# One fused attention and MLP kernel: its opening reordered, its queries computed one unit sooner, its V rows loaded in longer runs

## The chip, the cores and the metric

The kernel runs on one core of one Trainium2 chip. The metric is the device time of one execution in microseconds (us). The kernel before was run three times without the profiler: 1286.58, 1287.96 and 1288.90 us, median 1287.96. One more execution was taken by the hardware profiler; its time was 1287.13 us, and the span from its first to its last instruction 1285.4 us. All rows of the profile are from that execution.

## The reference, cut to what matters

```python
xn = layernorm(x)                                   # x: 2048 tokens x 512
# attention branch: 32 heads of 128, 2048 cached keys
q = (xn @ wq) split into heads
p = softmax((q @ k_cache.T) * 128 ** -0.5)          # per head, 2048 x 2048
s = (p @ v_cache) joined @ wo                       # 2048 x 512
# MLP branch, on the same xn
h  = gelu(layernorm(xn) @ w1); four column groups of h shifted by -1, +1, -2, +2 tokens
x1 = xn + shifted @ w2
g  = silu(x1 + gelu(layernorm(x1) @ w3) @ w4)
out = x + s * g
```

Inputs and output are bf16. Softmax is invariant to the order of the keys, as long as K and V use the same order.

## The kernel before, in words

**Tiling.** Attention is cut into 128 units. A unit is one head and 512 queries; the units run in groups of four heads, and inside a group over the four blocks of 512 queries, with the four heads innermost. So units 0 to 3 use tokens 0 to 511, units 4 to 7 tokens 512 to 1023, units 8 to 11 tokens 1024 to 1535, and units 12 to 15 tokens 1536 to 2047; then the next four heads start. A unit has eight slots. Slot number n counts through all units, so unit u begins with slot 8u. In each slot TensorE multiplies two blocks of 128 keys by the 512 queries (`s_slot`, L181, tile `ps_s`, two buffers), ScalarE takes the exponential of the 1024 results in one instruction (L191, tile `pT`), and TensorE does two matmuls of the exponentials with V for the slot five earlier (`pv_slot`, L210, tile `ps_o`). VectorE adds the eight exponential tiles of a unit (`add_first` L197, `add_next` L202, the folds L207 and L208), and TensorE turns that sum into the softmax denominators in slot 3 of the next unit (`sums`, tile `ps_sum`, four matmuls of one column). The reciprocal goes to DRAM and comes back spread over all partitions (`dr`, `rb`), and `norm` (L258) scales the unit's output.

**Queries.** `q_mm` (L165) makes the 512 queries of one unit: four matmuls from the transposed tokens `xnT` and the head's query weights `wq_h` into the PSUM tile `ps_q`; `q_copy` (L173) brings them to SBUF as `qT`. Units 1 to 3 get theirs during unit 0. From unit 3 on, unit u computes the queries of unit u + 1: two matmuls in its first slot, two in its second, the copy in its third.

**Tokens.** x is loaded in 16 tiles of 128 tokens. `ln1_stats` (L343) and `ln1_apply` (L360) normalise one tile: statistics on VectorE, a reciprocal square root on GpSimd (L117, L118), the scaling on VectorE (L355), then a DMA transpose issued by SyncE that writes the tile's part of `xnT`. The four tiles of the first 512 tokens are transposed on TensorE instead, by matmuls with an identity (`first_tokens`, L365). The other tiles have a fixed slot each for their statistics and their scaling, in two lists at L628 and L629: tiles 8 to 11 are scaled in slots 29, 37, 45 and 47, tiles 12 to 15 in slots 53, 61, 69 and 77.

**Order.** Every engine's instructions keep the order in which the program writes them (`pin`); there is no planner. Work tied to a slot is put into a list (`at`) and is written at the end of that slot. So an instruction that waits holds up all that stands behind it on its engine, and the DMAs issued by SyncE (SP) go out in one queue: K pieces (DMA transposes, four for each head), V halves, `dr`, `rb`, and the token transposes. The MLP branch is cut into 136 chunks that are spread over units 5 to 119. The output projection (`wo_mm`, tile `ps_wo`) takes four matmuls in a unit. In PSUM, `ps_q`, `ps_sum` and `ps_wo` share one buffer, and the MLP's `ps_m` has another.

**The end.** The last four token tiles' output projections go to four halves of two two-bank PSUM tiles, `pa` and `pb` (L738 to L740); each is scaled (L302), added (L307) and stored.

Of the kernel before, what the change touches and what calls it, by code (L numbers as in the profile page):

```python
# [17 lines left out]
def kernel(  # L18
# [15 lines left out]
    nc = tc.nc  # L34
# [77 lines left out]
    def mm(out, lhsT, rhs, start, stop):  # L112
        pin(nc.tensor.matmul(out=out, lhsT=lhsT, rhs=rhs, start=start, stop=stop))  # L113
# [15 lines left out]
    def at(n, fn):  # L129
        todo[n].append(fn)  # L130
# [16 lines left out]
                in_=A_k_cache[0, h, i * w:(i + 1) * w, :], transpose=True))  # L147

    def load_v(h, halves):
        v = A_v_cache[0, h].rearrange("(kc p) d -> p kc d", p=P)  # L150
        for i in halves:
            if i == 0:
                vBs[h] = vp.tile([P, KC, Dh], BF16, name="vb")
            ks = slice(i * KC // 2, (i + 1) * KC // 2)
            pin(nc.sync.dma_start(out=vBs[h][:, ks, :], in_=v[:, ks, :]))
# [9 lines left out]
    def q_mm(u, dcs):  # L165
        g, qt, hh = units[u]
        if dcs[0] == 0:
            st[u] = dict(psq=psX.tile([P, 512], FP32, tag="xa", name="ps_q"))
        for dc in dcs:
            mm(st[u]["psq"][:], wqs[g * HG + hh][:, dc, :],  # L170
               xnT[:, dc, qt * 512:(qt + 1) * 512], dc == 0, dc == DC - 1)

    def q_copy(u):  # L173
        qT = qtp.tile([P, 512], BF16, name="qT")
        if u > QUIET:
            pin(nc.scalar.activation(out=qT[:], in_=st[u].pop("psq")[:], func=ACT.Identity))
        else:
            pin(nc.vector.tensor_copy(out=qT[:], in_=st[u].pop("psq")[:]))  # L178
        st[u]["qT"] = qT

    def s_slot(u, p):  # L181
        g, qt, hh = units[u]
        s = st[u]
        sps = psS.tile([P, 2, 512], FP32, name="ps_s")
        for j in range(2):
            kc = 2 * p + j
            mm(sps[:, j, :], kTs[g * HG + hh][:, kc * P:(kc + 1) * P], s["qT"][:], True, True)
# [3 lines left out]
        pin(nc.scalar.activation(  # L191
            out=s["pT"][-1][:, jj:jj + 2, :], in_=sps[:], func=ACT.Exp, scale=SCALE))
# [167 lines left out]
    def ln1_apply(t):  # L360
        xn = ln1_norm(t)
        pin(nc.sync.dma_start_transpose(out=xnT[:, :, t * P:(t + 1) * P], in_=xn[:]))
        pin(nc.gpsimd.dma_start(out=xn_d[t][:], in_=xn[:]))

    def first_tokens():  # L365
        xns = [ln1_norm(t) for t in range(4)]
        st[0] = dict(psq=psX.tile([P, 512], FP32, tag="xa", name="ps_q"))
        psq = st[0]["psq"]
        for t in range(4):
            tp = psO.tile([P, DC, P], FP32, tag="ps_o", name="ps_o")  # L370
# [3 lines left out]
            pin(nc.scalar.activation(out=xnT[:, :, ts], in_=tp[:], func=ACT.Identity))  # L374
            if t >= 1:
                q_part(t - 1, psq)
        q_part(3, psq)
        qT = qtp.tile([P, 512], BF16, name="qT")
        pin(nc.vector.tensor_copy(out=qT[:, 0:3 * P], in_=psq[:, 0:3 * P]))
        pin(nc.vector.tensor_copy(out=qT[:, 3 * P:], in_=psq[:, 3 * P:]))  # L380
        st[0].pop("psq")
        st[0]["qT"] = qT
        for t in range(4):
            pin(nc.gpsimd.dma_start(out=xn_d[t][:], in_=xns[t][:]))

    def q_part(t, psq):
        ts = slice(t * P, (t + 1) * P)
        for dc in range(DC):
            mm(psq[:, ts], wqs[0][:, dc, :], xnT[:, dc, ts], dc == 0, dc == DC - 1)
# [223 lines left out]

    for t, eng in enumerate([nc.sync, nc.scalar, nc.sync, nc.scalar]):
        ln1_load(t, eng)
    for h in range(HG):
        load_w(h, nc.scalar)
    load_k(0, range(KSPLIT))
    load_v(0, (0, 1))
    load_k(1, range(KSPLIT))  # L620
    for t in range(4):
        ln1_stats(t)
    for t in range(4, 8):
        ln1_load(t, nc.gpsimd)
    first_tokens()
    load_v(1, (0, 1))
    load_k(2, (0, 1))
    for t, stats, apply in zip(range(4, NT), (2, 5, 8, 13, 23, 31, 39, 39, 47, 55, 63, 71),  # L628
                               (4, 7, 12, 15, 29, 37, 45, 47, 53, 61, 69, 77)):  # L629
        if t >= 8:  # L630
            at(stats - 8, lambda t=t: ln1_load(t, nc.gpsimd))
        at(stats, lambda t=t: ln1_stats(t))
        at(apply, lambda t=t: ln1_apply(t))
    for h, slots, halves in ((2, (2, 4), (9, 13)), (3, (5, 7, 14, 16), (21, 22))):
        for i, n in enumerate(slots):
            at(n, lambda h=h, i=i + KSPLIT - len(slots): load_k(h, (i,)))
        for i, n in enumerate(halves):
            at(n, lambda h=h, i=i: load_v(h, (i,)))
    at(28, ph1_load)
    at(64, w2_load)  # L640
    for h in range(HG):
# [146 lines left out]
```

## Time and profile before

| what | value |
|---|---|
| runs without profiler | 1286.58, 1287.96, 1288.90 us |
| profiled execution, its own time | 1287.13 us |
| span of the profiled execution | 1285.4 us |
| VectorE (DVE) busy | 1015.0 us, 79% of the span |
| ScalarE (ACT) busy | 1114.1 us, 87% |
| GpSimd (POOL) busy | 145.0 us, 11% |
| V halves (256 KB), issue to landing | 5.1 us median |
| K pieces, issue to landing | 5.0 us median |
| token transposes, issue to landing | 3.8 us median |

A busy share is a mean over the whole span. Matmul ends are modelled, so in a full stream one matmul of 512 columns shows as 379 ns, while the starts are about 216 ns apart. Where a row of the timeline merges several equal instructions, its first number is the start of the first one. What ended the idle time before an instruction stands in square brackets.

### The profile page before, as it was taken

How to read it: one execution, taken by the hardware profiler on the slowest of the kernel's cores; microseconds unless marked ns; L12 is line 12 of the kernel's file. 1: busy time of each engine (PE TensorE's matmuls, PEld its weight loads, DVE VectorE, ACT ScalarE, POOL GpSimd, SP SyncE). 2: the span in 40 equal slices, each digit the busy share in tenths (PEclk: the TensorE clock that was granted, in tenths of full speed). 3: DMA queues.
4: the chain of work that ended last, by engine and by line, in shares of the span. 5: the costliest groups of instructions: out<-in, count | busy, mean ns of one | idle time of the engine just before them, and what ended most of it. 6: DMA issues, size and time to landing. Idle time of an engine off the chain costs nothing.

```text
span 1285.4 us, 17152 instructions
## 1 busy us (share of the span) xinstructions
PE 1256.3 (98%) x6148; PEld 578.2 (45%) x6272; DVE 1015.0 (79%) x1390; ACT 1114.1 (87%) x1195; POOL 145.0 (11%) x253
## 2 busy tenths in 40 slices
PE   6999999999999999999999999999999999999998
PEld 3444444444444444444444444444444444444443
DVE  5888888888778777788787778887777888777895
ACT  5899998888999988899998889998888999888983
POOL 4432002333111110000001000000000000000110
PEclk9999999999999999999999999999999999999999
DMA  8645454366432554224464246622545224562522
GB/s 180 152 95 111 81 80 79 88 137 133 99 79 77 99 107 88 53 67 83 80 96 80 50 79 95 103 45 62 99 86 86 40 62 76 94 107 54 139 68 54
DMA packets 224791, 113.89 MB, mean 89 GB/s; under 512 B 192641, under 2 KB 201345, under 8 KB 224705
## 3 DMA queue, kind: packets, MB, share of 16 engines
q1 hardware_dynamic: 213056, 85.51, 36.2%
q0 software_dynamic: 9248, 26.49, 8.1%
q8 instruction: 49, 0.80, 0.3%
q10 hardware_dynamic: 2400, 0.79, 0.3%
q14 instruction: 38, 0.30, 0.1%
HBM read 82.58 MB, written 9.70 MB: 72 GB/s over the span
## 4 chain that ended last, share of the span: by engine, by line
PE 82%; ACT 9%; DVE 5%; issue 2%; DMA 1%; POOL 1%; SPq 0%; DVEq 0%; ACTq 0%; POOLq 0%
PE ps_s L113 30%; PE ps_o L113 28%; PE ps_m L113 9%; PE ps_wo L113 7%; PE ps_q L113 7%; ACT pT L191 6%; DVE acc L202 2%; ACT sq L399 1%; PE ps_sum L113 1%; ACT pre L429 1%; DVE acc L207 1%; DMA xin<-in_A_x_dram 0%; DMA kT<-in_A_k_cache_dram 0%; ACT sq L408 0%; DMA rb<-dr 0%
## 5 line engine op out<-in xcount | busy, mean ns | idle before, releaser
L191 ACT ACTIVATE pT<-ps_s 128x1024 bf16<-128x1024 f32 x1024 | 1012.9, 1030 | 145.5 <-PE ps_s L113 139.4
L113 PE MATMUL ps_s<-qT,kT 128*128 128x512 bf16 x2007 | 600.7, 379 | 4.5 <-ACT pT L191 0.9
L113 PE MATMUL ps_o<-pT,vb 128*128 128x512 bf16 x2007 | 599.7, 379 | 4.0 <-DMA vb<-in_A_v_cache_dram 1.6
L202 DVE TENSOR_TENSOR acc<-acc,pT 128x2048 bf16<-128x2048 bf16 x254 | 309.8, 1219 | 60.2 <-ACT pT L191 54.6
L113 PEld LDWEIGHTS <-vb 128*128 128x128 bf16 x2048 | 199.5, 98 | 243.3 <-DMA vb<-in_A_v_cache_dram 2.1
L113 PEld LDWEIGHTS <-kT 128*128 128x128 bf16 x2048 | 196.2, 98 | 239.2 <-issue 21.0
L197 DVE TENSOR_TENSOR acc<-pT 128x2048 bf16<-128x2048 bf16 x128 | 155.8, 1217 | 32.4 <-ACT pT L191 32.1
L113 PE MATMUL ps_q<-xnT,wq_h 128*128 128x512 bf16 (+1 forms) x512 | 151.4, 379 | 1.6 <-ACT xnT L374 0.9
L113 PE MATMUL ps_wo<-wo_h,oT 128*128 128x512 bf16 x450 | 134.8, 379 | 0.9 <-DVE rc L230 0.3
L325 DVE TENSOR_TENSOR s_acc<-ps_wo,s_acc 128x512 f32<-128x512 f32 x100 | 68.9, 689 | 80.3 <-PE ps_wo L113 74.8
L258 DVE TENSOR_TENSOR oT<-ps_o,rb 128x512 bf16<-128x512 f32 x129 | 87.2, 677 | 5.9 <-DMA rb<-dr 5.9
L207 DVE TENSOR_TENSOR acc<-acc 128x1024 bf16<-128x1024 bf16 x127 | 87.9, 692 | 4.3
L178 DVE CAST qT<-ps_q 128x512 bf16<-128x512 f32 x121 | 82.9, 685 | 3.9 <-PE ps_q L113 3.9
L113 PEld LDWEIGHTS <-wq_h 128*128 128x128 bf16 x524 | 51.8, 100 | 62.2 <-issue 3.1
L113 PEld LDWEIGHTS <-oT 128*128 128x128 bf16 x480 | 46.9, 98 | 58.2 <-issue 3.2
L113 PE MATMUL ps_m<-xn2T,w_sb 128*128 128x512 bf16 x217 | 65.0, 378 | 0.3
L113 PE MATMUL ps_m<-w_sb,h2T 128*128 128x512 bf16 x219 | 62.9, 379 | 0.3
L548 POOL DMA_DIRECT2D w_sb<-in_B_w_dram x28 | 21.1, 755 | 353.1 <-PE ps_m L113 313.2
L208 DVE TENSOR_TENSOR acc<-acc 128x512 bf16<-128x512 bf16 x127 | 54.0, 425 | 4.3
L230 DVE RECIPROCAL rc<-ps_sum 128x4 f32<-128x4 f32 x128 | 22.9, 179 | 37.7 <-PE ps_sum L113 36.9
L113 PEld LDWEIGHTS <-acc 128*128 128x128 bf16 x516 | 37.1, 116 | 34.7 <-DVE acc L208 6.6
L580 POOL DMA_DIRECT2D g_d<-xr x16 | 8.7, 546 | 343.0 <-DVE xr L578 343.0
(67 smaller groups left out, 595.0 us busy)
## 6 DMA issues: line engine op xcount, KB each, us to landing
rb<-dr SPq DMA_DIRECT2D x128, 256.0 KB, 4.4
vb<-in_A_v_cache_dram SPq DMA_DIRECT2D x64, 256.0 KB, 5.1
w_sb<-in_B_w_dram POOLq DMA_DIRECT2D x28, 256.0 KB, 4.2
wo_h<-in_A_wo_dram SPq DMA_DIRECT2D x32, 128.0 KB, 4.2
wq_h<-in_A_wq_dram SPq DMA_DIRECT2D x28, 128.0 KB, 4.5
kT<-in_A_k_cache_dram SPq DMA_TRANSPOSE x128, 5.0
xn_d<-xn POOLq DMA_DIRECT2D x16, 128.0 KB, 3.6
dr<-rc SPq DMA_DIRECT2D x128, 2.0 KB, 1.5
```

Source lines behind the costliest of these rows:

```text
L113: pin(nc.tensor.matmul(out=out, lhsT=lhsT, rhs=rhs, start=start, stop=stop))
L178: pin(nc.vector.tensor_copy(out=qT[:], in_=st[u].pop("psq")[:]))
L191: pin(nc.scalar.activation(out=s["pT"][-1][:, jj:jj + 2, :], in_=sps[:], func=ACT.Exp, scale=SCALE))
L197: pin(nc.vector.tensor_tensor(out=s["acc"][:], in0=s["pT"][0][:], in1=s["pT"][1][:], op=ALU.add))
L202: pin(nc.vector.tensor_tensor(out=a[:], in0=a[:], in1=st[u]["pT"][i][:], op=ALU.add))
L207: pin(nc.vector.tensor_tensor(out=a[:, 0:2, :], in0=a[:, 0:2, :], in1=a[:, 2:4, :], op=ALU.add))
L208: pin(nc.vector.tensor_tensor(out=a[:, 0, :], in0=a[:, 0, :], in1=a[:, 1, :], op=ALU.add))
L230: pin(nc.vector.reciprocal(out=rc[:], in_=ps[:]))
L258: pin(nc.vector.tensor_tensor(out=oTs[(g, qt)][:, hh, c], in0=s["o"][:, c], in1=s["rb"][:, c], op=ALU.mult))
L325: pin(nc.vector.tensor_tensor(out=sa, in0=ps[:], in1=sa, op=ALU.add))
L399: pin(nc.scalar.activation(out=sq[:], in_=pre[:], func=ACT.Square, scale=GELU_A ** 0.5))
L548: pin(nc.gpsimd.dma_start(out=w[:], in_=w3_v[:, :, fc * P:(fc + 2) * P]))
```

## The change

- ScalarE gets a first activation on one column right after its two loads of x.
- The query weights of heads 0 to 3 are loaded by GpSimd's queue, three of them before the statistics and one after, instead of by ScalarE's queue.
- TensorE starts with 48 matmuls of 128 columns of the identity with itself, into a score buffer.
- The four first token tiles are all transposed before any query matmul. Their copies out of PSUM are shared between ScalarE and VectorE, the last two tiles use score buffers, the first unit's queries lie in two PSUM tiles, and their copy is split between ScalarE and VectorE. The four stores of the normalised tiles go to slots 9 to 12.
- Statistics and scaling of token tiles 5 to 7 move to slots 5, 8, 11 and 9, 12, 14. The slots of tiles 8 to 15 stay.
- The K pieces of head 3 go to slots 11, 15, 17 and 19, the V halves of heads 2 and 3 to slots 11, 13 and 19, 20.
- From unit 3 on, unit u computes the queries of unit u + 2. Unit 4's queries are made in the last two slots of unit 2. The query weights of the next heads are loaded one unit sooner.
- V is read so that one partition holds four keys that follow each other in memory (1024 bytes instead of 256), and the score matmuls take every fourth column of K as their weights, so that both have the same key order.
- At the end the fourth projection goes to a PSUM tile of its own.

```diff
     def load_v(h, halves):
-        v = A_v_cache[0, h].rearrange("(kc p) d -> p kc d", p=P)
+        v = A_v_cache[0, h].rearrange("(i p j) d -> p i j d", p=P, j=KJ)
...
-            mm(sps[:, j, :], kTs[g * HG + hh][:, kc * P:(kc + 1) * P], s["qT"][:], True, True)
+            kv = kTs[g * HG + hh].rearrange("d (i p j) -> d i j p", p=P, j=KJ)
+            mm(sps[:, j, :], kv[:, kc // KJ, kc % KJ, :], s["qT"][:], True, True)
...
+    def warm_up(n):
+        wt = psS.tile([P, 2, 512], FP32, name="ps_s")
+        for _ in range(n):
+            mm(wt[:, 0, 0:P], ident[:], ident[:], True, True)
+
     def first_tokens():
         xns = [ln1_norm(t) for t in range(4)]
...
+        for t in range(3):
+            turn(t)
+            if t < 2:
+                back(t, (0, DC), True)
+            else:
+                back(t, (0, DC), False)
+        turn(3)
+        back(3, (0, 2), False)
+        back(3, (2, DC), True)
+        for t in range(3):
+            q_part(t)
+        pin(nc.scalar.activation(out=qT[:, 0:3 * P], in_=qA[:, 0:3 * P], func=ACT.Identity))
+        q_part(3)
+        pin(nc.vector.tensor_copy(out=qT[:, 3 * P:], in_=qB[:, 3 * P:]))
...
-    for h in range(HG):
-        load_w(h, nc.scalar)
+    act1 = const.tile([P, 1], FP32, name="act1")
+    pin(nc.scalar.activation(out=act1[:], in_=nhalf[:], func=ACT.Identity))
+    for h in range(HG - 1):
+        load_w(h, nc.gpsimd)
     load_k(0, range(KSPLIT))
     load_v(0, (0, 1))
     load_k(1, range(KSPLIT))
+    warm_up(WARM)
...
-    for t, stats, apply in zip(range(4, NT), (2, 5, 8, 13, 23, 31, 39, 39, 47, 55, 63, 71),
-                               (4, 7, 12, 15, 29, 37, 45, 47, 53, 61, 69, 77)):
+    for t, stats, apply in zip(range(4, NT), (2, 5, 8, 11, 23, 31, 39, 39, 47, 55, 63, 71),
+                               (4, 9, 12, 14, 29, 37, 45, 47, 53, 61, 69, 77)):
...
-            at((b + (-3, -3, 0, 0)[hh]) * SPU + (5, 7)[hh % 2], lambda h=h: load_w(h))
+            at((b + (-4, -4, -1, -1)[hh]) * SPU + (5, 7)[hh % 2], lambda h=h: load_w(h))
...
-        if p in (0, 1) and HG - 1 <= u < NU - 1:
-            q_mm(u + 1, (2 * p, 2 * p + 1))
+        if u == HG - 2 and p in (6, 7):
+            q_mm(HG, (2 * p - 12, 2 * p - 11))
+        if u == HG - 2 and p == 7:
+            q_copy(HG)
+        if p in (0, 1) and HG - 1 <= u < NU - 2:
+            q_mm(u + 2, (2 * p, 2 * p + 1))
...
-        if p == 2 and HG - 1 <= u < NU - 1:
-            q_copy(u + 1)
+        if p == 2 and HG - 1 <= u < NU - 2:
+            q_copy(u + 2)
...
-    dst = [(pa, pa, pb, pb)[j][:, j % 2, :] for j in range(4)]
+    pc = psX.tile([P, D], FP32, tag="xa", name="ps_wo")
+    dst = [pa[:, 0, :], pa[:, 1, :], pb[:, 0, :], pc[:]]
```

More of the change, by code (lines that the diff above doesn't have):

```diff
@@ L56 @@
     KSPLIT = 4
+    KJ = KC // KSPLIT
     BASE_J = [3, 3, 2, 2]
@@ L59 @@
     PADW = 8
+    WARM = 48
     PSUM = bass.MemoryType.PSUM
@@ L153, in load_v @@
                 vBs[h] = vp.tile([P, KC, Dh], BF16, name="vb")
-            ks = slice(i * KC // 2, (i + 1) * KC // 2)
-            pin(nc.sync.dma_start(out=vBs[h][:, ks, :], in_=v[:, ks, :]))
+            ks = slice(i * KSPLIT // 2, (i + 1) * KSPLIT // 2)
+            pin(nc.sync.dma_start(
+                out=vBs[h].rearrange("p (i j) d -> p i j d", j=KJ)[:, ks], in_=v[:, ks]))
     def load_w(h, eng=nc.sync):
@@ L167, in q_mm @@
         if dcs[0] == 0:
-            st[u] = dict(psq=psX.tile([P, 512], FP32, tag="xa", name="ps_q"))
+            st[u] = dict(psq=psX.tile([P, 512], FP32, tag="xm" if u == HG else "xa", name="ps_q"))
         for dc in dcs:
@@ L174, in q_copy @@
         qT = qtp.tile([P, 512], BF16, name="qT")
-        if u > QUIET:
+        if u > QUIET + 1:
             pin(nc.scalar.activation(out=qT[:], in_=st[u].pop("psq")[:], func=ACT.Identity))
@@ L363, in ln1_apply, with turn @@
         pin(nc.gpsimd.dma_start(out=xn_d[t][:], in_=xn[:]))
+    def warm_up(n):
+        wt = psS.tile([P, 2, 512], FP32, name="ps_s")
+        for _ in range(n):
+            mm(wt[:, 0, 0:P], ident[:], ident[:], True, True)
     def first_tokens():
         xns = [ln1_norm(t) for t in range(4)]
[L367 to L370, printed above, removed]
+        st[0] = {}
+        qA = psX.tile([P, 512], FP32, tag="xa", name="ps_q")
+        qB = psX.tile([P, 512], FP32, tag="xm", name="ps_q")
+        qT = qtp.tile([P, 512], BF16, name="qT")
+        st[0]["qT"] = qT
+        tps = []
+        def turn(t):
+            if t < 2:
+                tp = psO.tile([P, DC, P], FP32, tag="ps_o", name="ps_o")[:]
+            else:
+                tp = psS.tile([P, 2, 512], FP32, name="ps_s")[:, 0, :].rearrange("p (c q) -> p c q", c=DC)
@@ L371, in first_tokens @@
             for dc in range(DC):
                 mm(tp[:, dc, :], xns[t][:, dc * P:(dc + 1) * P], ident[:], True, True)
-            ts = slice(t * P, (t + 1) * P)
[L374 to L380, printed above, removed]
@@ L381, in first_tokens, with back @@
-        st[0].pop("psq")
-        st[0]["qT"] = qT
-        for t in range(4):
[L384 to L389, printed above, removed]
+            tps.append(tp)
+        def back(t, dcs, on_act):
+            dst = xnT[:, dcs[0]:dcs[1], t * P:(t + 1) * P]
+            src = tps[t][:, dcs[0]:dcs[1], :]
+            if on_act:
+                pin(nc.scalar.activation(out=dst, in_=src, func=ACT.Identity))
+            else:
+                pin(nc.vector.tensor_copy(out=dst, in_=src))
@@ new lines, in q_part @@
+        def q_part(t):
+            ts = slice(t * P, (t + 1) * P)
+            psq = qB if t == 3 else qA
+            for dc in range(DC):
+                mm(psq[:, ts], wqs[0][:, dc, :], xnT[:, dc, ts], dc == 0, dc == DC - 1)
+        for t in range(3):
+            turn(t)
+            if t < 2:
+                back(t, (0, DC), True)
+            else:
+                back(t, (0, DC), False)
[4 more added lines that the diff above has]
+            q_part(t)
@@ L392 @@
+        pin(nc.scalar.activation(out=qT[:, 0:3 * P], in_=qA[:, 0:3 * P], func=ACT.Identity))
+        q_part(3)
+        pin(nc.vector.tensor_copy(out=qT[:, 3 * P:], in_=qB[:, 3 * P:]))
+        for t in range(4):
+            at(9 + t, lambda t=t: pin(nc.gpsimd.dma_start(out=xn_d[t][:], in_=xns[t][:])))
     mlp = {}
@@ L620 @@
     load_k(1, range(KSPLIT))
+    warm_up(WARM)
     for t in range(4):
         ln1_stats(t)
+    load_w(HG - 1, nc.gpsimd)
     for t in range(4, 8):
@@ L633 @@
         at(apply, lambda t=t: ln1_apply(t))
[L634 to L638, printed above, removed]
+    for n, h, piece in ((2, 2, 2), (4, 2, 3), (11, 3, 0), (15, 3, 1), (17, 3, 2), (19, 3, 3)):
+        at(n, lambda h=h, piece=piece: load_k(h, (piece,)))
+    for n, h, half in ((11, 2, 0), (13, 2, 1), (19, 3, 0), (20, 3, 1)):
+        at(n, lambda h=h, half=half: load_v(h, (half,)))
     at(28, ph1_load)
@@ L664 @@
             pv_slot(*divmod(m, SPU))
-        if u == 0 and p in (0, 2, 4):
+        if u == 0 and p in (1, 3, 5):
             q_mm(1 + p // 2, range(DC))
-        if u == 0 and p in (1, 3, 5):
-            q_copy(1 + p // 2)
-        if p in (0, 1) and HG - 1 <= u < NU - 1:
-            q_mm(u + 1, (2 * p, 2 * p + 1))
+        if u == 0 and p in (2, 4, 6):
+            q_copy(p // 2)
+        if u == HG - 2 and p in (6, 7):
[4 more added lines that the diff above has]
+            q_mm(u + 2, (2 * p, 2 * p + 1))
         if p == 0 and u >= 1:
             add_last(u - 1)
-        if p == 2 and HG - 1 <= u < NU - 1:
-            q_copy(u + 1)
+        if p == 2 and HG - 1 <= u < NU - 2:
+            q_copy(u + 2)
         if p == 2 and u >= 2:
```

## The prediction

> **What bounds the kernel now.** I read the page's busy shares first, then a table of windows, then the timeline where the windows lose time.
>
> ```profile
> PE 1256.3 (98%) x6148; PEld 578.2 (45%) x6272; DVE 1015.0 (79%) x1390; ACT 1114.1 (87%) x1195; POOL 145.0 (11%) x253
> ```
>
> ```profile
> 0.00:10.00 10.00, 1.69 (x15) 1.53 (x16) 4.83 (x15) 2.37 (x3) 5.11 (x16) 1.00 0.87 178
> 10.00:20.00 10.00, 8.78 (x40) 4.49 (x39) 2.92 (x6) 5.05 (x6) 3.66 (x8) 1.00 1.19 244
> 20.00:30.00 10.00, 8.91 (x45) 3.83 (x43) 8.67 (x14) 8.89 (x11) 4.19 (x6) 1.00 0.63 138
> 40.00:60.00 20.00, 18.33 (x90) 8.29 (x91) 16.39 (x28) 17.40 (x20) 7.72 (x20) 1.00 0.60 146
> 60.00:80.00 20.00, 19.66 (x97) 8.97 (x97) 17.90 (x28) 18.34 (x21) 6.97 (x9) 1.00 0.46 98
> 320.00:640.00 320.00, 317.95 (x1553) 146.24 (x1582) 251.56 (x330) 287.70 (x312) 25.64 (x43) 1.00 0.41 83
> ```
>
> The columns after the window are the busy us of PE, weight loads, DVE, ACT and POOL, the granted clock, the DMA share and GB/s. From 60 us on PE is short of nothing (317.95 of 320). So the time is PE's work plus what PE loses before 60 us and at the end: whatever PE waits less in the opening is gained in full, and a wait put in later is lost in full.
>
> ```profile
> 7.40 1.28 ACT L374 ACT_TABLE_LOAD   x1 [7.40 <-DMA kT<-in_A_k_cache_dram]
> 13.33 1.01 PE L113 MATMUL ps_s<-qT,kT 128*128 128x512 bf16 x2 [0.85 <-DVE qT L380]
> 14.13 1.91 PE L113 MATMUL ps_q<-xnT,wq_h 128*128 128x512 bf16 x4
> 15.84 1.91 PE L113 MATMUL ps_s<-qT,kT 128*128 128x512 bf16 x4
> 17.55 1.09 PE L113 MATMUL ps_q<-xnT,wq_h 128*128 128x512 bf16 x4
> 19.10 8.36 ACT L191 ACTIVATE pT<-ps_s 128x1024 bf16<-128x1024 f32 x9 [0.23 <-PE ps_s L113]
> 27.79 0.29 PE L113 MATMUL ps_sum<-ones_t,acc 128*128 128x1 bf16 x4 [1.09 <-DVE acc L208]
> 36.40 0.29 PE L113 MATMUL ps_sum<-ones_t,acc 128*128 128x1 bf16 x4 [1.15 <-DVE acc L208]
> 47.55 0.60 PE L113 MATMUL ps_o<-pT,vb 128*128 128x512 bf16 x2 [1.57 <-DMA vb<-in_A_v_cache_dram]
> ```
>
> The first score matmul stands at 13.33. From there to 17.55 a matmul takes (15.84 - 14.13) / 4 = 0.427 us, later 0.216, though the clock column says 1.00: PE starts at half rate. The Trainium skill ("TensorE: Matmul & The Clock Gate", Part 1) has the clock at half until about 3.4 us of sustained work; the full-rate row at 17.55 agrees, 4.2 us after 13.33. Then come three waits, two for a unit's sum and one for V of head 3.
>
> The price of the query change is read further on. Slots 44 to 47 carry, behind scores and PV, two projection and two MLP pairs; the next query pair is the first of slot 48.
>
> ```profile
> 66.82 2.73 SPq L362 DMA_TRANSPOSE xnT<-xn  x2
> 67.92 0.41 DVE L355 TENSOR_SCALAR xn<-xin,mv,rs 128x512 bf16<-128x512 bf16 x1
> 69.43 0.59 PE L113 MATMUL ps_q<-xnT,wq_h 128*128 128x512 bf16 x2
> DMA to landing us min/median/max: 3.6/3.9/4.2
> ```
>
> ```profile
> 104.96 0.41 DVE L355 TENSOR_SCALAR xn<-xin,mv,rs 128x512 bf16<-128x512 bf16 x1
> 105.78 1.20 SPq L362 DMA_TRANSPOSE xnT<-xn  x1
> 106.20 3.18 POOL L461 DMA_DIRECT2D xr<-xn_d  x6
> 109.24 0.59 PE L113 MATMUL ps_q<-xnT,wq_h 128*128 128x512 bf16 x2
> DMA to landing us min/median/max: 6.4/6.4/6.4
> ```
>
> The DVE rows are token tiles 11 (slot 47) and 15 (slot 77); the PE rows are the query pairs of slots 48 and 80; the last line of each fence is from the tile view of these transposes.
>
> **The change part by part**
>
> *Ledger of the opening before.* Up to slot 48 (its scores start at 68.57) PE has 96 score, 86 PV, 24 query, 4 projection and 8 MLP matmuls, 218 x 0.2157 = 47.0, and five groups of sums, 0.7. So 68.57 - 47.7 = 20.9 us are lost: 13.3 before the first score; half rate, ten matmuls in 4.22 instead of 2.16, 2.1; the three waits, start to start, 1.25 + 1.31 + 1.72 = 4.3; the rest 1.2.
>
> *Start, -2.6.* The scaled tiles 0 to 3 end at about 7.6, 7.9, 8.2 and 8.85; their loads and statistics do not change. ACT's table load (1.28) moves to about 1.6 and lies beside the wait for x. Tile 3 is turned by 9.3. DVE copies tile 2 (0.69, by the 512-column CAST rows) and half of tile 3 (0.42), to 9.8. The last query part, 0.25 with its tail, and DVE's copy of 128 columns (0.28) end near 10.7. Bounds: 10.4, and 11.8 if PE is at half rate or the weights come late. Those take three POOL issues of 0.54 to 0.76 (rows of POOL loads) before the first square root at 4.98, so POOL is free by 3.4, and land about 4.2 us after issue, as POOL's w_sb does: needed at 9.1, hidden. The fourth delays the loads of tiles 4 to 7 by one issue; they are needed two slots and more after the start.
>
> *Half rate, -2.1.* The 48 extra matmuls take 48 x 0.107 (rows of 128 columns at 7.63, eight in 1.04 with the tail) = 5.1 us, in time in which PE waits. Bounds: -2.1, and 0 if they do not suffice.
>
> *The two sum waits, -2.4 of 2.6.* Before, DVE's last add for unit 0 stood behind the scaling of tile 5, which waited for POOL. Now it stands right behind the add before it. Exponentials come 0.904 apart (nine in 8.36). Sum's chain: 1.25 + 0.72 + 0.42 = 2.4 after the last exponential of the unit; PE reaches it 2.7 after. I leave 0.2. Bounds: 0 and 1.
>
> *V, and SP's queue, -0.7 of 1.7.* K and V are issued earlier relative to need, but need comes earlier too. The tight item is token tile 7, which unit 4's queries need in slot 22, about 32.0. Ahead of its transpose SP issues 13 K pieces (1.31), six V halves (0.62), three transposes (1.25), `dr` and `rb` (0.9), from 1.64 on: 27.0, plus up to 4.4 for blocked issues and the wait for `dr`; landing 3.6 later, 30.6 to 35.0. I take a wait of 1.0, nearer the low end, since V now has a quarter of the packets; bounds 0 and 3.
>
> *The rest, -0.2.* With PE waiting less, ACT sets the pace up to slot 22: PE's slot without queries is 4 x 0.2157 = 0.863 against 0.904. PE gets there 20.4 after the first score with 19.7 of work; with 0.3 for unit 3 that is 1.0 instead of 1.2. The four token stores that move to slots 9 to 12 use idle POOL.
>
> Opening in all: -2.6 - 2.1 - 2.4 - 0.7 - 0.2 = -8.0.
>
> *Unit 8's queries, +2.5.* They move from slot 56 to slot 48, but need tile 11, scaled in slot 47 as before. In the rows its transpose is issued at 68.36 and lands 3.6 later, at 71.95, while PE stands there at 69.43. Behind it on PE stands everything, so the wait is a loss. Bounds by the landings of `xnT` up to 80 us (2.8 to 6.7): 1.7 to 5.6.
>
> *Unit 12's queries, +2.6.* Slot 80 instead of 88, tile 15 of slot 77: issued 105.78, landed 6.4 later at 112.1, PE there at 109.24, so 2.9. Beside it ran POOL's six loads, which stay, and two query weights at 107.03, which now go out earlier; I take 0.3 off. Bounds: 0.1 (landing in 3.6) and 2.9. From unit 13 on all tokens are there.
>
> *Strided K weights, 0.* Nothing before has them in a score matmul, but the sums load `acc` with the same step of four: 115 ns instead of 98, and still 33 ns from start to start, and the PV matmul beside the first of them keeps 0.216. So they hide under 0.216. The Trainium skill (same page, Weight-path perf modes) keeps the fast load for column steps up to 1,024; by that the sum is the same.
>
> *End, +0.5 and -0.45.* Unit 127 has no query pairs now, and loses 0.8 around its sums at 1262.5; unit 126 becomes such a unit (0 to 0.9). Of the last scalings the third waited 0.44 for PE, which was busy with the fourth in the same tile; that wait goes.
>
> Sum: -8.0 + 2.5 + 2.6 + 0.5 - 0.45 = -2.85. On the profiled execution's 1287.13 that is 1284.3; it lay 0.8 below the median of the runs, 1287.96, so 1285.1 there.
>
> **The rivals**
>
> *Short query waits.* The transposes land in 2.8 and 3.6: 0.8 and 2.5 less, 1281.8. For it: tiles 8 and 9 landed so; against it: six loads run beside tile 15 in both kernels.
>
> *The opening's work does not do what it says.* PE stays at half rate (2.1, and 0.4 in the start): 1287.6. For it: the matmuls between 7.63 and 13.33, with gaps, did not bring full rate before 17.55, and after the extra ones there is a gap of about 1 us and then gaps again.
>
> *PE falls back to half rate after the two query waits: slower.* The longest later wait before, 1.57, kept 0.216 afterwards. Waits of 2.5 to 2.9 have no row. A fall costs at least the 2.1 of the first stretch, at most half of 7.63 to 17.55, 5.0; two at 3 give 1291.1. It decides from 2.85 lost in all. The Trainium skill (same page, the table "Why this matters for your kernels") warns of PE gaps above about 3 us; by that both waits just escape, and the time stays at 1285.1. No run here shows it yet.
>
> *The strided weights show.* 17 ns on 2048 loads, 35 us: 1320. It decides from 1.4 ns a load. Against it: the 33 ns of the sums.
>
> **How the numbers follow.** Forecast 0.43, short waits 0.20, half rate kept 0.18, half rate again 0.14, strided weights 0.05. A change below 0.2%, 2.6 us, is about what a measurement of this kernel can't tell from none; the bounds are 1285.4 and 1290.5. The forecast's own range, 1282.8 to 1287.2, lies a bit more than half below 1285.4. Faster: 0.24 + 0.20 = 0.44. Slower: 0.10 of the half-rate case and 0.05, 0.15. The same: 0.41. The range 1281 to 1290.5 leaves out part of the short waits and the slow cases, 0.2.
>
> **What would show it.** Right: first score at 10.4 to 11, its successors 0.216 apart; no sum wait over 0.3 before 40 us; PE waiting 2 to 3 us for `xnT` near 61 and near 104 us, then 0.216 again; kT weight loads near 115 ns, and scores 0.216 apart. Wrong: half-rate matmuls after 20 us, query waits under 1 or above 4 us, or V and K waits in the first 45 us above 2.

## The result, and the profile after

The changed kernel takes 1292.76 us, the median of five executions between 1290.41 and 1294.11; the kernel before takes 1287.96 (five executions, 1286.58 to 1288.90). The ratio is 1.0037, with a 95% interval from 1.0022 to 1.0051: slower, where 1285.1 was forecast. The profiled execution took 1290.41 us, 2.35 less than the median, so the trace shows one of the milder cases; it is 3.28 above the profiled execution of before.

The page's line of busy shares and the table of windows (us of PE, weight loads, DVE, ACT, POOL, granted clock, DMA share, GB/s), of the changed kernel:

```profile
PE 1267.2 (98%) x6320; PEld 612.3 (48%) x6320; DVE 1016.6 (79%) x1392; ACT 1114.5 (86%) x1195; POOL 146.0 (11%) x257
...
L115 PEld LDWEIGHTS <-kT 128*128 128x128 bf16 x2048 | 226.9, 113 | 224.6 <-issue 19.1
```

```profile
0.00:10.00 10.00, 7.02 (x78) 6.36 (x79) 5.77 (x17) 3.00 (x6) 7.80 (x19) 1.00 0.87 177
10.00:20.00 10.00, 9.22 (x43) 4.32 (x43) 6.76 (x12) 8.48 (x10) 3.30 (x8) 1.00 1.23 243
20.00:30.00 10.00, 9.74 (x47) 4.40 (x45) 9.02 (x16) 10.00 (x12) 6.42 (x12) 1.00 0.62 141
30.00:40.00 10.00, 6.88 (x34) 3.19 (x35) 5.12 (x9) 5.67 (x7) 0.29 (x1) 1.00 0.92 200
60.00:80.00 20.00, 18.01 (x91) 8.51 (x88) 15.95 (x24) 16.71 (x19) 5.32 (x7) 1.00 0.36 80
100.00:120.00 20.00, 17.10 (x77) 7.62 (x76) 13.49 (x20) 14.66 (x16) 6.31 (x11) 0.91 0.37 87
320.00:640.00 320.00, 319.64 (x1579) 153.96 (x1578) 252.54 (x332) 287.29 (x312) 25.53 (x43) 1.00 0.41 85
```

(PE's counts and busy times of the two pages can't be compared: that of before lacks 124 matmul records, 6148 against 6272 weight loads.) From 320 to 640 us PE is full, 319.64 of 320. Time is lost in three earlier places. The stretch from 30 to 40 us has 3.1 us of idle PE. That from 60 to 80 has 2.0, and that from 100 to 120 has 2.9 and a granted clock of 0.91. PE's timeline shows the first of them:

```profile
10.75 1.03 PE L115 MATMUL ps_s<-qT,kT 128*128 128x512 bf16 x4 [0.48 <-DVE qT L419]
11.61 1.03 PE L115 MATMUL ps_q<-xnT,wq_h 128*128 128x512 bf16 x4
...
30.21 0.29 PE L115 MATMUL ps_sum<-ones_t,acc 128*128 128x1 bf16 x4 [0.47 <-DVE acc L212]
...
33.95 0.59 PE L115 MATMUL ps_o<-pT,vb 128*128 128x512 bf16 x2 [2.13 <-DVE oT L262]
...
36.19 0.59 PE L115 MATMUL ps_q<-xnT,wq_h 128*128 128x512 bf16 x2 [0.78 <-DMA vb<-in_A_v_cache_dram]
```

The first score stands at 10.75 (before: 13.33), and four matmuls take 0.86: full rate from the first score on. The row at 36.19 names a V load, but what ended that wait is the transpose of tile 7, issued at 30.18 and landed 5.9 us later. At 33.95 there is a wait that before did not have. PV of unit 2 wants its PSUM tile `ps_o`, of which there are two, and unit 0 still holds one until its norm (L262) has multiplied by the broadcast reciprocals `rb`. The timeline from 22 us, of SP's queue and that norm, shows why it is late:

```profile
23.22 1.21 SPq L366 DMA_TRANSPOSE xnT<-xn  x1
24.53 0.52 SPq L236 DMA_DIRECT2D dr<-rc  x1
25.11 1.18 SPq L147 DMA_TRANSPOSE kT<-in_A_k_cache_dram  x1
26.34 0.58 SPq L157 DMA_DIRECT2D vb<-in_A_v_cache_dram  x1
27.78 0.34 SPq L251 DMA_DIRECT2D rb<-dr  x1
33.21 0.69 DVE L262 TENSOR_TENSOR oT<-ps_o,rb 128x512 bf16<-128x512 f32 x1 [3.06 <-DMA rb<-dr]
```

The reciprocals are ready at 23.1. Their store `dr` stands behind the transpose of tile 5, goes out at 24.53 and lands at 27.7; only then can `rb` go out, and it takes 5.3 us, beside V, K, two more transposes of tokens and the eight token transfers that POOL issued from 23.9 to 29.1. It is a round trip of 10 us where PE allows 8: the two scores ahead start at 31.23, so the tile is wanted near 31.7, and the norm takes 0.69.

In the kernel before the same trip took 7.5 us (reciprocals at 28.5, `rb` landed at 36.0) and cost nothing: PE stood at a sum until 36.40 and wanted the tile only at 37.84, 0.9 us after the norm's end. Rows of SP's queue and of the norm before:

```profile
28.90 0.52 SPq L232 DMA_DIRECT2D dr<-rc  x1
32.56 0.34 SPq L247 DMA_DIRECT2D rb<-dr  x1
36.26 0.68 DVE L258 TENSOR_TENSOR oT<-ps_o,rb 128x512 bf16<-128x512 f32 x1
```

The other two places are the waits for queries that the prediction had. Timeline rows of slots 47/48 and of slots 77/80:

```profile
64.93 0.41 DVE L359 TENSOR_SCALAR xn<-xin,mv,rs 128x512 bf16<-128x512 bf16 x1
65.37 1.19 SPq L366 DMA_TRANSPOSE xnT<-xn  x1
68.60 0.59 PE L115 MATMUL ps_q<-xnT,wq_h 128*128 128x512 bf16 x2 [1.99 <-DVE acc L212]
...
104.74 1.22 SPq L366 DMA_TRANSPOSE xnT<-xn  x1
110.94 0.74 PE L115 MATMUL ps_q<-xnT,wq_h 128*128 128x512 bf16 x2 [2.61 <-DVE acc L211]
111.48 1.06 PE L115 MATMUL ps_s<-qT,kT 128*128 128x512 bf16 x2
```

The page names DVE, which had long been done: the transposes landed at 68.51 and 110.85, just ahead of PE. Start to start, less the 0.216 of a matmul, the waits cost 2.15 and 2.77 us. Behind the second, two score matmuls take 1.06 and not 0.59, and a window there has the clock:

```profile
111.40:114.60 3.20, 3.20 (x9) 1.19 (x8) 0.32 (x1) 1.02 (x1) 0.54 (x1) 0.50 0.25 82
115.00:118.00 3.00, 3.00 (x19) 1.54 (x18) 2.55 (x4) 2.73 (x4) 0.00 (x0) 1.00 0.02 1
```

In the ledger of this execution, by equal work: -3.85 up to slot 48 (its scores start at 65.58 in place of 68.57, and four query matmuls more are done, 0.86), +1.9 at slot 48, +4.4 at slot 80 with 1.7 of half rate in it, and +0.75 behind that, the end above all. That makes +3.2 of the 3.28.

### The profile page after: what moved, and what is told of

Same layout as the page of the kernel before. It is cut to its first block, busy times and chain, and to the rows that moved or that the text cites. A ratio compares the mean times of both kernels' runs of the same rounds, so it can differ in the third digit from the quotient of the medians.

```text
span 1288.6 us, 17369 instructions
## 1 busy us (share of the span) xinstructions
PE 1267.2 (98%) x6320; PEld 612.3 (48%) x6320; DVE 1016.6 (79%) x1392; ACT 1114.5 (86%) x1195; POOL 146.0 (11%) x257
## 2 busy tenths in 40 slices
DMA packets 173718, 113.89 MB, mean 88 GB/s; under 512 B 125056, under 2 KB 150144, under 8 KB 173632
## 4 chain that ended last, share of the span: by engine, by line
PE 85%; ACT 7%; DVE 5%; DMA 1%; issue 1%; POOL 0%; DVEq 0%; SPq 0%; ACTq 0%; POOLq 0%
PE ps_s L115 31%; PE ps_o L115 29%; PE ps_m L115 9%; PE ps_wo L115 8%; PE ps_q L115 7%; ACT pT L195 5%; DVE acc L206 2%; PE ps_sum L115 1%; ACT sq L431 1%; DMA xin<-in_A_x_dram 1%; ACT pre L461 1%; DVE acc L211 1%; DMA vb<-in_A_v_cache_dram 0%; DVE bn L351 0%; DVE qT L181 0%
## 5 line engine op out<-in xcount | busy, mean ns | idle before, releaser
L115 PE MATMUL ps_s<-qT,kT 128*128 128x512 bf16 x2048 | 609.6, 379 | 2.0 <-ACT pT L195 0.7
L115 PE MATMUL ps_o<-pT,vb 128*128 128x512 bf16 x2048 | 609.1, 379 | 2.1 <-DVE oT L262 2.1
L115 PEld LDWEIGHTS <-kT 128*128 128x128 bf16 x2048 | 226.9, 113 | 224.6 <-issue 19.1
L115 PE MATMUL ps_wo<-wo_h,oT 128*128 128x512 bf16 x468 | 138.8, 379 | 0.0
L262 DVE TENSOR_TENSOR oT<-ps_o,rb 128x512 bf16<-128x512 f32 x129 | 87.2, 676 | 6.1 <-DMA rb<-dr 6.1
```

Of the source, the lines that this page charges most:

```text
L262: pin(nc.vector.tensor_tensor(out=oTs[(g, qt)][:, hh, c], in0=s["o"][:, c], in1=s["rb"][:, c], op=ALU.mult))
```

## The experiments

All times are medians; each stands beside runs of the kernel before on the same chip at the same time.

| kernel | us | before | ratio (95%) |
|---|---|---|---|
| one_ahead | 1284.74 | 1287.29 | 0.9980 (0.9971 to 0.9989) |
| tokens_earlier | 1283.66 | 1287.29 | 0.9970 (0.9960 to 0.9979) |
| fill_waits | 1293.08 | 1287.29 | 1.0043 (1.0031 to 1.0056) |
| before_two_ahead | 1292.22 | 1287.29 | 1.0041 (1.0028 to 1.0054) |
| te_stores_later | 1282.61 | 1288.07 | 0.9960 (0.9947 to 0.9972) |
| te_stores_back | 1282.55 | 1288.07 | 0.9957 (0.9944 to 0.9969) |
| te_dr_first | 1282.10 | 1288.07 | 0.9955 (0.9943 to 0.9968) |
| te_kv_slots_old | 1285.77 | 1288.07 | 0.9981 (0.9971 to 0.9990) |
| clear_path | 1280.49 | 1286.50 | 0.9953 (0.9941 to 0.9966) |
| clear_path_tokens_late | 1286.88 | 1286.50 | 1.0005 (0.9996 to 1.0014) |
| clear_path_tokens_late_fill | 1287.02 | 1286.50 | 1.0004 (0.9996 to 1.0013) |
| clear_path_no_warm | 1281.22 | 1286.50 | 0.9958 (0.9945 to 0.9972) |
| clear_path_layout_old | 1285.50 | 1287.33 | 0.9984 (0.9975 to 0.9993) |
| clear_path_one_ahead | 1282.37 | 1287.33 | 0.9957 (0.9945 to 0.9970) |

### The two waits for queries

**one_ahead**: the queries go back to one unit ahead, the rest stays changed.

```diff
-        if u == HG - 2 and p in (6, 7):
-            q_mm(HG, (2 * p - 12, 2 * p - 11))
-        if u == HG - 2 and p == 7:
-            q_copy(HG)
-        if p in (0, 1) and HG - 1 <= u < NU - 2:
-            q_mm(u + 2, (2 * p, 2 * p + 1))
+        if p in (0, 1) and HG - 1 <= u < NU - 1:
+            q_mm(u + 1, (2 * p, 2 * p + 1))
...
```

> The changed kernel with the queries one unit ahead again (their slots, copies, ring tag and weight loads as before), all else as changed. Theory A (the two waits for tiles 11 and 15, 2.3 us at slot 48 and 2.96 us at slot 80, less some 0.2 of normal spacing each, and half rate behind them, 1.7 us in the profiled execution and more in the other executions, are the whole loss outside the opening): both waits vanish, the granted clock goes from 0.995-0.997 to 0.998 or more, and the time falls by 4.9 of waits and 1.7 to 4 of rate, to 1285 to 1287 us. Theory B (the loss sits in the opening's new waits, 2.1 for ps_o at 33.95 us, and in the strided layout or the tail): the time falls by the waits alone, if those only hide another limit by nothing, 1290 to 1293. In both the ps_o wait near 34 us stays, within 0.5 us.

**tokens_earlier**: the queries stay two ahead, and their tokens come sooner.

```diff
-    ... (2, 5, 8, 11, 23, 31, 39, 39, 47, 55, 63, 71),
-        (4, 9, 12, 14, 29, 37, 45, 47, 53, 61, 69, 77)):
+    ... (2, 5, 8, 11, 23, 31, 33, 37, 47, 55, 63, 67),
+        (4, 9, 12, 14, 29, 37, 39, 43, 53, 61, 69, 73)):
```

> The changed kernel, queries still two units ahead, with the statistics and scaling of tiles 10, 11 and 15 four to six slots earlier (tile 10 at 33/39, tile 11 at 37/43, tile 15 at 67/73). Theory A: xnT of tile 11 lands some 4.5 us earlier and so before slot 48, that of tile 15 as well before slot 80; both waits go, and with them the half rate: 1285 to 1287 us, within 1 us of the kernel with one unit ahead. If the extra work of VectorE in slots 33 to 43 delays the sums there, up to 1 us comes back. Theory B: 1290 to 1293.

**before_two_ahead**: the kernel before, with the queries two units ahead (their copies and weight loads with them) and nothing else of the change.

> The kernel before with only the queries moved two units ahead (slots, copies, ring tag of unit 4, weight loads), the opening, K, V and token slots as before. Theory A: the two waits appear as in the changed kernel, 2.1 and 2.8 us, with half rate behind the second or both: 4.9 and 1.7 to 4 more than before, less up to 1 us for queries that no longer stand in front of their own unit's scores: 1292 to 1296 us. Theory B: 1288 to 1290.

All three agree with theory A in what happens: the two waits are gone from the traces of the first two, and both are there in the third. The times of the first two, 1284.7 and 1283.7, lie below A's 1285 to 1287. The queries two ahead cost the kernel before 4.9 us (1292.22 against 1287.29), against 5.1 in the prediction; its trace has 2.12 and 2.66 for the two waits, and a wait of 1.39 for queries near 41 us in place of the 1.72 for V. The timeline of `before_two_ahead` has the two, and this execution shows full rate behind them:

```profile
73.41 0.59 PE L113 MATMUL ps_q<-xnT,wq_h 128*128 128x512 bf16 x2 [1.95 <-DVE acc L208]
...
115.61 0.61 PE L113 MATMUL ps_q<-xnT,wq_h 128*128 128x512 bf16 x2 [2.50 <-DMA xnT<-xn]
```

So theory A's half rate is not bound to come. And the `ps_o` wait, expected to stay within 0.5 us of the changed kernel's 2.13, is no constant: 1.72 in `one_ahead`, but 3.56 in `tokens_earlier`, whose profiled execution took 1286.78 where its shortest took 1282.78, with half rate behind it. A row of its PE timeline, and a window behind that:

```profile
35.40 1.01 PE L115 MATMUL ps_o<-pT,vb 128*128 128x512 bf16 x2 [3.56 <-DVE oT L262]
```

```profile
36.00:38.00 2.00, 2.00 (x6) 0.67 (x5) 1.77 (x2) 0.70 (x1) 0.00 (x0) 0.50 0.60 122
```

**fill_waits**: PE is kept at work through both waits; the products are overwritten by the queries.

```diff
+        if p == 0 and u + 2 in FILL:        # FILL = {8: 36, 12: 44}
+            wf = psX.tile([P, 512], FP32, tag="xa", name="ps_q")
+            st[u + 2] = dict(psq=wf)
+            for _ in range(FILL[u + 2]):
+                mm(wf[:, 0:P], ident[:], ident[:], True, True)
...
```

> The changed kernel with 36 and 44 identity matmuls of 128 columns (0.053 us each at full rate: 1.9 and 2.35 us) put ahead of the queries of units 8 and 12, into the same PSUM tile that the queries then overwrite; the waits for tiles 11 and 15 themselves stay. Theory A1 (an idle TensorE is what brings the half rate): the score behind both waits keeps the 0.216 us spacing in every execution, granted clock 0.998 or more, and the time falls by what the half rate cost, 1.7 us against the profiled execution and 2 to 4 against the median: 1288 to 1291. Theory A2 (the half rate comes from something else, such as a governor over the whole execution): the clock stays 0.995 to 0.997 and the time 1291 to 1294, or longer if the added matmuls do not fit in the waits.

This settled nothing as a time: behind both fills the rate was full, but the `ps_o` wait ahead of them was 3.86 us in the profiled execution and brought 6.8 us of half rate of its own. The comparison had to wait for a kernel without that wait.

### The wait for ps_o

These four start from `tokens_earlier`, and each moves one thing near `rb`. **te_stores_later** and **te_stores_back** move the first four tiles' stores (`at(9 + t, ...)`) to slots 24 to 27 or right behind the first tokens; **te_dr_first** moves the scaling of tile 5 from slot 9 to slot 11, so that `dr` goes ahead of its transpose; **te_kv_slots_old** gives K of unit 3 and V of units 2 and 3 the slots they had before the change.

> The kernel with tokens 10, 11 and 15 earlier (1283.7 us, 1282.8 to 1286.8), and the stores of the first four scaled tiles at slots 24 to 27 in place of 9 to 12. Theory C (the wait for ps_o near 34 us, 2 to 4 us and half rate behind it when it is long, is the broadcast rb of unit 0 held up by the seven token transfers that GpSimd issues at 23.9 to 29.6 us, four of them these stores): rb lands 1.5 to 2.5 us earlier, near 31; the ps_o wait falls under 0.8 us, the half rate behind it is gone, the wait for the sum near 30.2 (0.84 us, GpSimd's square root of tile 7 behind two of the stores) falls to 0.3: 1280.5 to 1282.0. Theory D (rb is late because of its place on SP's queue and K and V around it, the stores weigh nothing): 1283 to 1285, the wait stays at 2 to 4 us.

> The same kernel with the four stores issued right behind the first tokens, as before the change. Theory C: as for the later stores, the ps_o wait under 0.8 us and 1280.5 to 1282.5, unless the 512 KB collide with V and K of unit 1 there (landing at 18 to 22 us), which would show as a wait for vb or kT before 25 us, up to 1 us. Theory D: 1283 to 1285.

> The same kernel with the scaling and turning of tile 5 at slot 11 in place of 9, so that on SP the store dr of unit 0's reciprocals goes out ahead of xnT of tile 5, 1.3 us earlier (23.2 us in place of 24.5). Theory C: rb is then issued 1.3 us earlier but still meets the stores; the ps_o wait shortens by 0 to 1.3 us: 1282 to 1283.5. Theory D (SP's queue): it shortens by 1.3 us or more, and the half rate behind it goes: 1281 to 1282.5.

> The same kernel with K of unit 3 at slots 5, 7, 14, 16 and V of units 2 and 3 at 9, 13 and 21, 22, as before the change (long runs and strided weights kept). Theory C: V of unit 3 arrives late again (before: 1.7 us of wait near 47.6), rb of unit 0 meets less at 30 us but the two K pieces are ahead of it on SP: the ps_o wait changes by under 1 us, and the total is 1283 to 1286. Theory D: with two fewer transfers of K and V between dr and rb, the ps_o wait falls under 0.8: 1281 to 1283 less nothing for V.

Neither theory holds alone. With the stores moved, the wait for the sum at 30.2 is gone in both traces, as theory C said (tile 7's square root stood behind them on POOL), but the `ps_o` wait is still near 1.7, and not under 0.8. With `dr` first it falls to 0.9, and the sum wait stays. To judge these waits: the four traces that leave the whole trip as in the changed kernel have 1.9 to 4.0, start to start, from one execution to the next. So the fall to 0.9 is clear, and that to 1.7 is just outside. By the medians each gains some 2 us against the kernel before over what `tokens_earlier` has (-5.5, -5.5 and -6.0 against -3.6); the intervals of the ratios still overlap. The old slots of K and V don't help, against theory D: the median is 2.3 below the kernel before where `tokens_earlier` has 3.6, and the wait is 3.53 against 3.56. Two K transposes more stand on SP ahead of `dr`, which goes out at 26.54, `rb` at 30.97. The late V that theory C expected there did not show.

```profile
26.54 0.44 SPq L236 DMA_DIRECT2D dr<-rc  x1
30.97 0.34 SPq L251 DMA_DIRECT2D rb<-dr  x1
...
35.08 0.77 PE L115 MATMUL ps_o<-pT,vb 128*128 128x512 bf16 x2 [3.53 <-DVE oT L262]
```

**clear_path** does all of it: tokens earlier, `dr` first, stores later, and V of unit 2 ahead of `dr`.

```diff
-    for n, h, piece in (..., (11, 3, 0), (15, 3, 1), (17, 3, 2), (19, 3, 3)):
+    for n, h, piece in (..., (13, 3, 0), (15, 3, 1), (17, 3, 2), (19, 3, 3)):
-    for n, h, half in ((11, 2, 0), (13, 2, 1), (19, 3, 0), (20, 3, 1)):
+    for n, h, half in ((6, 2, 0), (7, 2, 1), (19, 3, 0), (20, 3, 1)):
...
```

> The changed kernel with four groups of slots moved: tiles 10, 11 and 15 earlier, tile 5 at slot 11 (behind dr on SP), the first four stores at slots 24 to 27, and V of unit 2 at slots 6 and 7 with K of unit 3 at 13, 15, 17, 19, so that only dr, xnT of tile 5 and rb stand on SP from 23 us on. Theory E (the ps_o wait is the sum of a queue on SP and of traffic beside rb, and all of it can be cleared): dr at 23.0, rb issued by 25 and landed by 30 us; no ps_o wait (0 to 0.3), the wait for unit 4's queries 0 to 1.2, the sum's wait at 30.2 0.2 to 0.8: 1279.5 to 1281.0. Theory F (rb lands late whatever is around it, 5 us after issue, or the wait moves on to the next buffer or to unit 4's queries): 1281.5 to 1283.

Theory E holds in the time and in the wait, which is gone; `rb` was issued at 26.8 and not by 25, since `dr` took 3.8 us to land. Timeline rows of `clear_path`:

```profile
22.99 0.42 SPq L236 DMA_DIRECT2D dr<-rc  x1
26.82 0.34 SPq L251 DMA_DIRECT2D rb<-dr  x1
30.26 0.69 DVE L262 TENSOR_TENSOR oT<-ps_o,rb 128x512 bf16<-128x512 f32 x1 [1.11 <-PE ps_s L115]
32.70 0.59 PE L115 MATMUL ps_q<-xnT,wq_h 128*128 128x512 bf16 x2 [0.24 <-DMA xnT<-xn]
```

The norm now waits for nothing from DMA. At 1280.49 this kernel beats both: 6.0 us below the kernel before, and its five executions lie within 0.8 us.

### What the parts are worth once the path is clear

**clear_path_tokens_late** puts tiles 10, 11 and 15 back into the changed kernel's slots; **clear_path_tokens_late_fill** adds the 36 and 44 filling matmuls to that.

> The kernel with the cleared path and the token tiles 10, 11 and 15 in the changed kernel's slots, so that the two waits for queries at slots 48 and 80 stand alone, without the ps_o wait ahead of them. Theory A: 2.1 and 2.8 us of waits and 1.7 to 4 of half rate more than the cleared path, 5 to 8.5 us. Against it: if the two waits are shorter here or hidden, under 4.

> The same as the last, with 36 and 44 identity matmuls of 128 columns ahead of the queries of units 8 and 12 into the tile that these overwrite. Theory A1 (TensorE's idleness brings the half rate): 1.5 to 3.5 us less than without them, with a spread between executions of under 1.5 us, score spacing 0.216 us behind both waits. Theory A2 (the clock falls for another reason): no less, or longer by up to 0.5.

The two waits with what follows them cost 6.4 us (1286.88 against 1280.49), inside theory A's range. The fill kept the rate: its mean granted clock is 0.999 or 1.0 in all executions but one, against 0.995 to 1.0 without. But the median did not fall, so theory A1 holds for the clock and fails for the time. In the two profiled kernels with fills the transpose of tile 11 took 4.8 and 5.0 us from issue to landing, in the three without that had this wait (the changed kernel, `before_two_ahead`, `clear_path_tokens_late`) 3.1 to 3.2. That of tile 15, under the longer fill, took 5.7 and 5.8 us, and 5.8 to 6.1 without. Whether the filling matmuls lengthen tile 11's stays open.

**clear_path_no_warm** has `WARM = 0`.

> The cleared path with no identity matmuls at the start (48 of them taken out). If these are what brings the full rate forward: scores at half rate from the first, 0.427 us apart, until about 3.4 us of work have gone by, and 1.5 to 2.5 us more in all, less what the opening's later waits absorb. If the rate rises by itself: within 0.3 us of the cleared path.

It lies between the two: 0.73 us more. PE's timeline shows half rate from the first transposed tile on, but without gaps, and full rate from 12.5:

```profile
8.95 1.91 PE L115 MATMUL ps_q<-xnT,wq_h 128*128 128x128 bf16 x16
11.34 1.57 PE L115 MATMUL ps_s<-qT,kT 128*128 128x512 bf16 x4 [0.47 <-DVE qT L419]
12.75 1.03 PE L115 MATMUL ps_q<-xnT,wq_h 128*128 128x512 bf16 x4
```

So full rate comes 5.2 us earlier than in the kernel before (12.48 against 17.66 in the clock record) without them, from turning the tiles back to back. Leaving the 48 matmuls out costs 1.2 us at slot 0, of which the waits between 31 and 50 us take back 0.7.

**clear_path_layout_old** takes back V in long runs and the strided K weights, **clear_path_one_ahead** the queries two units ahead.

> The cleared path with V in rows of 128 keys as before (short runs, four times the packets of V) and the K weights contiguous again; only this part of the change is undone. Theory G (strided weights cost nothing, as the prediction has it, and V's layout matters only where V is late, which the earlier slots have settled): 1280 to 1281.5 against the cleared path's 1280.5, ratio to the kernel before 0.994 to 0.997, kT weight loads 98 ns in place of 113 to 115, score spacing 0.216 in both. Theory H (the shorter packets slow V and the broadcasts that share the DMA queues): a wait for vb, or ps_o waits over 1 us, in the first 50 us: 1282 to 1284.

> The cleared path with the queries one unit ahead again, the early tiles kept. If queries two units ahead gain something by themselves once their tiles are there: 0.5 to 2 us longer than the cleared path, with waits for sums or queries in units 1 to 12. If the order of the queries has no worth of its own: within 0.5 us, 1280 to 1281, ratio to the kernel before 0.994 to 0.9965.

Of the three parts taken back the layout is worth most: 1285.50 against 1287.33 is -1.8, where the cleared path has -6.0. Theory H holds in sign and in the `ps_o` wait; the time lies above its 1282 to 1284. The V halves of unit 2 go out ahead of `dr` in both kernels. In short runs (222870 packets in all and not 173718) they land at 27.2 and 28.4 in place of 25.1 and 26.2, and `dr`, which goes out 1.9 us later, lands behind them at 28.9. Most of that is the issue on SP and not the trip: the V halves of units 0 and 1 hold the queue for 1.97 and 2.39 us a pair in place of 1.10 and 1.09 in the cleared path. Of `dr`'s 1.9 us, 0.5 are the later start of this execution and 1.4 this queue. Timeline rows of SP with these V halves, of the cleared path and then of this kernel:

```profile
6.81 1.10 SPq L157 DMA_DIRECT2D vb<-in_A_v_cache_dram  x2
13.09 1.09 SPq L157 DMA_DIRECT2D vb<-in_A_v_cache_dram  x2
```

```profile
6.81 1.97 SPq L157 DMA_DIRECT2D vb<-in_A_v_cache_dram  x2
14.38 2.39 SPq L157 DMA_DIRECT2D vb<-in_A_v_cache_dram  x2
```

The `ps_o` wait is back, with half rate from 33.5 to 36.9:

```profile
24.89 0.81 SPq L234 DMA_DIRECT2D dr<-rc  x1
28.97 0.35 SPq L249 DMA_DIRECT2D rb<-dr  x1
33.85 1.01 PE L115 MATMUL ps_o<-pT,vb 128*128 128x512 bf16 x2 [2.37 <-DVE oT L260]
```

Theory G holds for the weights alone: 113 ns a load against 98 (the page's rows of both), yet from the exponential of slot 290 to that of slot 1010 the cleared path takes 883.36 us and this kernel 883.25.

One unit ahead costs about 1 us by the ratios (-5.0 against -6.0), less than the intervals can tell; the trace agrees in sign. Slot 48 comes 1.2 later, or 2.1 by equal work, since four query matmuls fewer (0.86) are done by then; a `ps_o` wait of unit 3 near 42 us, 2.4, brings it. At the end 0.5 comes back. What two units ahead is worth by itself stays at that.

## Why the prediction was wrong

*Start, -2.6, and half rate, -2.1.* First score at 10.75 as forecast, and scores 0.216 apart. The cause was only half right: without the extra matmuls the same opening loses 1.2 of the 4.7; the rest comes from the new order of the opening, whose gapless turning brings full rate by itself at 12.48.

*The two sum waits, -2.4.* They brought -1.9: the first went; at 30.2 the second kept 0.6 of its 1.31, start to start. The working followed DVE's chain and missed that tile 7's scaling waits for POOL.

*V, and SP's queue, -0.7.* This is the step that failed. Its own items came out right (tile 7's wait 0.9 for 1.0, V's wait gone), but it counted SP's queue only for tile 7 and for V. `dr` and `rb` stood in that sum as 0.9 us of issue, and nobody asked who waits for them. The answer, norm and with it the second-next unit's `ps_o`, costs 2.3 us start to start in this execution and up to 4 in others. The sentence that the four moved stores "use idle POOL" failed with it: POOL was idle in busy time, but they went in front of tile 7's square root, and their traffic lay beside `rb`. `dr` sent ahead of one transpose cut the wait to 0.9, clearing the whole trip took it away, and V in short runs brought it back. So the opening brought 3.85 and not 8.0; with the path clear it is 6.8 on the same count (slot 48's scores 5.90 earlier, plus 0.86).

*The rest, -0.2.* It grew instead, by the same ledger from 1.2 to 2.4. The largest pieces are 0.5 before a score at 13.37, which waited for an exponential, and 0.8 and 0.3 before sums at 59.85 and 42.57, where the page names VectorE's copy of queries. No run takes these apart.

*Unit 8's and unit 12's queries, +2.5 and +2.6.* Right: 2.15 and 2.77 in the trace, and 4.9 when the queries two ahead are the only change to the kernel before.

*Half rate after the query waits.* It was a rival at 0.14, and the time, 1290.41 profiled and 1292.76 in the median, lies around its 1291.1. That the number fits is in part luck: it has two falls at 3 on an opening of -8.0, and the trace has one fall at 1.7 on an opening of -3.85. The rival was given too little: the argument that one wait of 1.57 had kept the rate said nothing of 2.5. The price was lower than its 2.1 to 5.0 a fall: 3.41 us at half rate are 1.7 lost. The other four executions are 1.2 to 3.7 us longer, with a mean granted clock of 0.995 or 0.996 against 0.997. By an estimate from these clocks, 1.3 to 2.6 us of that are more half rate: 0.001 of 1290 us is 2.6 us at half rate, of which half is lost.

*Strided K weights, 0.* Right. *V in long runs*, with the strided weights that go with it, was worth 3.4 us (profiled executions) to 4.2 us (medians against before) on the cleared path, where "a quarter of the packets" was a reason for the lower end of one wait.

*End, +0.5 and -0.45.* Unit 126's sum wait is there, 0.47 start to start. The third scaling's wait went too, but nothing came of it. Timeline rows of DVE at the end of the kernel before, then of the changed kernel, then POOL's of the changed kernel:

```profile
1280.15 1.29 DVE L302 SCALAR_TENSOR_TENSOR gf<-ps_s,gf 128x512 bf16<-128x512 f32 x2 [0.44 <-PE ps_s L113]
1281.35 1.28 DVE L307 TENSOR_TENSOR xf<-gf,s_acc 128x512 bf16<-128x512 bf16 x2
```

```profile
1281.37 1.89 DVE L306 SCALAR_TENSOR_TENSOR gf<-ps_s,gf 128x512 bf16<-128x512 f32 x3 [1.12 <-PE ps_s L115]
1283.17 0.68 DVE L306 SCALAR_TENSOR_TENSOR gf<-ps_wo,gf 128x512 bf16<-128x512 f32 x1
1283.77 1.80 DVE L311 TENSOR_TENSOR xf<-gf,s_acc 128x512 bf16<-128x512 bf16 x2
```

```profile
1282.14 2.27 POOL L311 TENSOR_TENSOR xf<-gf,s_acc 128x512 bf16<-128x512 bf16 x2 [35.45 <-DVE gf L306]
```

DVE's adds now start at 1283.77, while POOL's second add runs until 1284.41, and the pair takes 1.80 and not 1.28: the first of them 1.20. What was gained at 0.44 was given back at 0.52. That POOL's add slows DVE's is read from this overlap; no run separates it.

## What to carry to other kernels

When work is pulled earlier, price every buffer that must come free by then, with the whole trip that frees it: here a 2 KB store, its landing, and a broadcast on a queue that other parts of the same change had filled. A tuned queue has no idle place that can be seen in busy time; ask of each transfer that is put there what is issued behind it and who waits for that. And read several executions: a wait near a threshold of the clock costs more in one and nothing more in the next.

## What was not expected of the hardware

The granted clock changes on a grid that runs by itself. In the trace's clock record the time from the first full rate to the first fall is 105.81 us in the changed kernel, 27.31 in `tokens_earlier`, `fill_waits` and `clear_path_layout_old`, 30.72 in `te_kv_slots_old` and 61.44 in `clear_path_tokens_late`: 31, 8, 9 and 18 times 3.413. The falls last 3.41 or 6.83. Where the grid lies differs from one execution to the next: in the 13 kernels that start with the 48 matmuls the first full rate comes at 4.63 to 7.29 us. The Trainium skill ("TensorE: Matmul & The Clock Gate", Part 1, "What's actually happening") gives a free-running window of 3413 ns; the trace agrees.

By the same grid, counting in each window the time in which PE had no matmul (0.22 us from each start counted as work), at full rate and among 512-column matmuls:

| idle in one window, us | the next window |
|---|---|
| 3.13, 2.78, 2.77, 2.53, 2.24, 2.19 | half rate |
| 2.12, 2.12, 2.11, 1.83, 1.81, 1.81 and less | full rate |

So it is not the wait's length that decides but how much of it falls into one window. The second wait of `before_two_ahead`, 2.65 us without a matmul, fell into two windows, whose idle time came to 1.6 and 1.3, and cost nothing more, while the 2.24 us of the first wait of `clear_path_tokens_late` lay in one window and brought half rate. Since the grid's phase changes from one execution to the next, the same wait costs 1.7 us more or not. The Trainium skill's rule in the same place, half rate after an idle window, and its limit of about 3 us on a gap (section "Why this matters for your kernels"), by which the prediction had both waits escape, are too lenient here: 2.2 us in one window are enough.

The 128-column matmuls at the start fit in, if each counts as the 0.056 us from one start to the next: 2.17 us idle in a window brought half rate (`te_stores_later`, a fall from 8.2 to 11.6), 2.10 did not (`te_dr_first`). The way up follows the same grid, with each matmul of the opening counted at its length at half rate: windows with 0.93 us idle or more were followed by half rate again, those with 0.70 or less by full rate. The kernel before had 1.09 and 1.55 in the two windows from 7.42 to 14.25, and so full rate only at 17.66; `clear_path_no_warm` had 0.68.
